# Decode attention over a long KV cache on one core: K in 16 KB rows, K and V on one transfer queue, a third V buffer

## The chip, the cores and the metric

One core of a Trainium2 chip. The metric is the device time of one execution in microseconds; medians of several executions are given. The before and after kernels were profiled in the same state, and no run of this case was in the slow state, besides three of the four of one failed experiment (10).

## The reference, cut to what matters

```python
B, Sq, D = 8, 4, 448
Hq, Hkv, Sk, Dh = 16, 8, 8192, 256          # bf16 throughout
q = (x @ wq) split into heads                # [B, Hq, Sq, Dh]
scores = einsum("bhqd,bhkd->bhqk", q, k) * Dh**-0.5     # k, v repeated twice over the heads
p = softmax(scores); o = einsum("bhqk,bhkd->bhqd", p, v)
out = o.reshape(B, Sq, Hq * Dh) @ wo
```

There are 64 pairs of batch and kv head ("heads" below). Each brings 4 MB of K and 4 MB of V that are read once: 537 MB in all, for 8 queries a head. So it is a streaming problem.

## The kernel before

Per head, TensorE transposes K in 16 groups of 512 keys (T), VectorE and ScalarE copy the transposed group out of PSUM (E), and TensorE multiplies it with the queries (QK, 3 groups later). A head behind, the softmax runs in small steps (D1 to D5, A1, P3 to P5), and then PV multiplies V with the probabilities.

```python
# SP: K in 16 slots of 512 KB, 4 KB a partition
for KGi in range(NH * 8):
    if n >= 1: eng.wait_ge(sem_T, 2 * (KGi - RK) + 2)        # slot consumed
    eng.dma_start(Kring[slot][:], k_cache[b, hkv]...[:, kg * 8 : (kg + 1) * 8, :]).then_inc(sem_kslot[slot], 16)
...
# ACT: V, two buffers, two transfers of 2 MB, 16 KB a partition
def Vdma(i):
    if i >= 2: eng.wait_ge(sem_pmisc, pm(i - 2, 4))          # PV of head i-2 done
    for q in range(2): eng.dma_start(Vbuf[i % 2][...], ...).then_inc(sem_v[i % 2], 16)
...
# TensorE: order of work
for G in range(NG + LAG):
    T(G); QK(G - LAG)
    # from group 9 of the next head on: PV of the last head, in pieces of 18 to 20 matmuls
```

Of the kernel before, what the change touches and what calls it, by code (L numbers as in the profile page):

```python
# [10 lines left out]
TG = 16  # L11
NG = NH * TG
KG_PER_HEAD = 8
RK = 16
RT = 6
NTB = 4
LAG = 3
SCALE = DH ** -0.5
NV_DMA = 2
# [12 lines left out]
def bass_standalone__gqa_block_cached__sampling_kernel(  # L32
# [24 lines left out]
    def dm(j, k):  # L57
        return 8 * j + k

    def pm(j, k):  # L60
        return 4 * j + k

    PV_SLOTS = {9: (0, 10), 10: (10, 19), 11: (19, 28), 12: (28, 37), 13: (37, 46), 14: (46, 55), 15: (55, 64)}

    with ExitStack() as ctx:
        Kring = [ctx.enter_context(nc.sbuf_tensor(f"Kr{s}", [128, 8, DH], bf16)) for s in range(RK)]
        Vbuf = [ctx.enter_context(nc.sbuf_tensor(f"Vb{s}", [128, NCH, DH], bf16)) for s in range(2)]
        KT = [ctx.enter_context(nc.sbuf_tensor(f"KT{s}", [128, 1024], bf16)) for s in range(RT)]
        wq_sb = ctx.enter_context(nc.sbuf_tensor("wq_sb", [128, 4, 2048], bf16))
        wo_sb = ctx.enter_context(nc.sbuf_tensor("wo_sb", [128, 32, D], bf16))  # L70
# [17 lines left out]
        tb16 = [tbank[t][:, :].bitcast(bf16) for t in range(NTB)]  # L88
        Sbank = [ctx.enter_context(nc.psum_tensor(f"Sb{t}", [128, 512], fp32)) for t in range(2)]
        misc = ctx.enter_context(nc.psum_tensor("misc", [128, 512], fp32))  # L90
        proj = ctx.enter_context(nc.psum_tensor("proj", [128, 512], fp32))
        misc16 = misc[:, 0:128].bitcast(bf16)
        S1_16 = Sbank[1][:, 0:64].bitcast(bf16)

        def pmaxT_ap(jp):
            return misc16[0:8, jp * 128 : (jp + 1) * 128]

        def bcast_ap(jp):
            return misc[:, 128 + jp * 8 : 128 + jp * 8 + 8]

        def oacc_ap(jp):
            return misc[:, 192 + jp * 16 : 192 + jp * 16 + 16]

        sem_kslot = [ctx.enter_context(nc.semaphore(f"sem_kslot{s}")) for s in range(RK)]
        sem_v = [ctx.enter_context(nc.semaphore(f"sem_v{s}")) for s in range(2)]
# [8 lines left out]
        sem_wqA = ctx.enter_context(nc.semaphore("sem_wqA"))  # L114
        sem_wqB = ctx.enter_context(nc.semaphore("sem_wqB"))
# [15 lines left out]
        @block.sync  # L131
        def _(eng):
            for KGi in range(NH * KG_PER_HEAD):
                i, kg = divmod(KGi, KG_PER_HEAD)
                hkv, b = _head(i)
                slot = KGi % RK
                n = KGi // RK
                if n >= 1:
                    eng.wait_ge(sem_T, 2 * (KGi - RK) + 2)
                src = k_cache[b, hkv].rearrange("(p c) d -> p c d", p=128)[:, kg * 8 : (kg + 1) * 8, :]  # L140
                eng.dma_start(Kring[slot][:], src).then_inc(sem_kslot[slot], 16)
            eng.wait_ge(sem_fin, 1)
            eng.dma_start(out.flatten_outer_dims(), out_sb[:]).then_inc(sem_out, 16)
            eng.wait_ge(sem_out, 16)

        @block.gpsimd
        def _(eng):
            eng.dma_start(x_sb[:], x.flatten_outer_dims()).then_inc(sem_x, 16)
            eng.dma_start(
                wq_sb[:, 0:3, :], wq[0:384, 0:2048].rearrange("(dc p) n -> p dc n", p=128)  # L150
            ).then_inc(sem_wqA, 16)
            eng.dma_start(wq_sb[0:64, 3, :], wq[384:448, 0:2048]).then_inc(sem_wqA, 16)
# [7 lines left out]
            eng.wait_ge(sem_qproj, 1)  # L160
            eng.dma_start(
                wq_sb[:, 0:3, :], wq[0:384, 2048:4096].rearrange("(dc p) n -> p dc n", p=128)
            ).then_inc(sem_wqB, 16)
            eng.dma_start(wq_sb[0:64, 3, :], wq[384:448, 2048:4096]).then_inc(sem_wqB, 16)
            eng.dma_start(wo_sb[:], wo.rearrange("(k p) n -> p k n", p=128)).then_inc(sem_wo, 16)

        @block.tensor
        def _(eng):
# [12 lines left out]
            def qproj(X):  # L181
                eng.wait_ge(sem_wqA if X == 0 else sem_wqB, 32)
# [3 lines left out]
                for hl in range(8):  # L186
                    for hf in range(2):
                        r = hl * 2 + hf
                        for dc in range(4):
# [3 lines left out]
                                wq_sb[0:w, dc, hl * 256 + hf * 128 : hl * 256 + (hf + 1) * 128],  # L193
# [5 lines left out]
            def outproj(hkv):  # L199
                eng.wait_ge(sem_dmisc, dm(hkv * B + B - 1, DM_D6))  # L200
                if hkv == 0:
                    eng.wait_ge(sem_wo, 16)
                    eng.wait_ge(sem_qt, 2)
                for hrep in range(2):
                    for hf in range(2):
# [4 lines left out]
                            wo_sb[:, k, :],  # L210
                            start=(k == 0), stop=(k == 31),
                        )
                if hkv == HKV - 1:
                    ins.then_inc(sem_outp, 1)

            def T(G):
                i, g = divmod(G, TG)
                KGi = i * KG_PER_HEAD + g // 2
                slot = KGi % RK
                if G % 2 == 0:  # L220
                    eng.wait_ge(sem_kslot[slot], 16 * (KGi // RK + 1))
                if G >= NTB:
                    s_, cnt = esem(G - NTB)
                    eng.wait_ge(s_, cnt)
                tb = tb16[G % NTB]
                for jj in range(4):
                    cc = (g % 2) * 4 + jj
                    for half in range(2):
                        r = jj * 2 + half
# [8 lines left out]
            def QK(G):  # L238
                i, g = divmod(G, TG)
                hkv, b = _head(i)  # L240
                s_, cnt = esem(G)
                eng.wait_ge(s_, cnt)
                if g == 0:
                    if i >= 2:
                        eng.wait_ge(sem_dmisc, dm(i - 2, DM_D5A))
# [8 lines left out]
                for jj in range(4):  # L254
                    c = g * 4 + jj
                    for half in range(2):
                        r = jj * 2 + half
# [8 lines left out]
            def P3(j):  # L266
                jp = j % 2
                eng.wait_ge(sem_dmisc, dm(j, DM_D1))
                if j >= 1:
                    eng.wait_ge(sem_dmisc, dm(j - 1, DM_D6))  # L270
                eng.matmul(pmaxT_ap(jp), pmax_sb[jp][:, 0:8], ident[:, :], is_transpose=True).then_inc(sem_pmisc, 1)  # L271

            def P4(j):
                jp = j % 2
                eng.wait_ge(sem_dmisc, dm(j, DM_D3))
# [7 lines left out]
            def PV(j, c0, c1):  # L283
                jp = j % 2
                hkv, b = _head(j)
                if c0 == 0:
                    eng.wait_ge(sem_v[jp], 16 * NV_DMA * (j // 2 + 1))
                    if j >= 1:
                        eng.wait_ge(sem_dmisc, dm(j - 1, DM_D6))
                ins = None  # L290
                for idx in range(c0 * 2, c1 * 2):
# [3 lines left out]
                        Vbuf[jp][:, c, half * 128 : (half + 1) * 128],  # L295
# [3 lines left out]
                if c1 == NCH:  # L299
                    ins.then_inc(sem_pmisc, 1)  # L300

            for G in range(NG + LAG):
                i, g = divmod(G, TG)
                j = i - 1
                if G < NG:
                    T(G)
                if G == 2:
                    qproj(0)
                if G == 16:
                    qproj(1)  # L310
                if G >= LAG:
                    QK(G - LAG)
                if j >= 0 and j < NH:
                    if g == 4:
                        P3(j)
                    elif g == 6:
                        P4(j)
                    elif g == 9:
                        P5(j)
                    if g in PV_SLOTS:  # L320
                        c0, c1 = PV_SLOTS[g]
                        PV(j, c0, c1)
                    if g == 2 and j >= B and (j % B) == 0:
                        outproj(j // B - 1)
            j = NH - 1
            P3(j)
            P4(j)
            P5(j)
            for g in range(9, 16):
                c0, c1 = PV_SLOTS[g]  # L330
                PV(j, c0, c1)
            outproj(HKV - 1)

        @block.vector
        def _(eng):
# [29 lines left out]
            def D2D3(j):  # L365
                jp = j % 2
                eng.wait_ge(sem_pmisc, pm(j, 1))
                eng.tensor_reduce(gmax_sb[0:8, jp : jp + 1], pmaxT_ap(jp), AX.X, ALU.max).then_inc(sem_dmisc, 1)  # L368
                eng.wait_ge(sem_dmisc, dm(j, DM_D2))
# [4 lines left out]
            def D4(j):  # L374
                jp = j % 2
                eng.wait_ge(sem_pmisc, pm(j, 2))
                eng.tensor_copy(bcast_sb[jp][:, :], bcast_ap(jp)).then_inc(sem_dmisc, 1)
                eng.wait_ge(sem_dmisc, dm(j, DM_D4A))
# [9 lines left out]
            def D5(j):  # L388
                jp = j % 2
                eng.wait_ge(sem_pmisc, pm(j, 3))  # L390
# [3 lines left out]
                eng.wait_ge(sem_dmisc, dm(j, DM_D5A))  # L394
                eng.reciprocal(linv_sb[jp][:, :], lsum_sb[jp][:, :]).then_inc(sem_dmisc, 1)  # L395

            def D6(j):
                jp = j % 2
                hkv, b = _head(j)
                eng.wait_ge(sem_pmisc, pm(j, 4))  # L400
                eng.wait_ge(sem_dmisc, dm(j, DM_D5B))
# [12 lines left out]
            for G in range(NG + TG):  # L414
                i, g = divmod(G, TG)
                j = i - 1
                if G < NG and not evac_is_act(G):
                    E_dve(G)
                if G == 3:
                    qt_evac(0)  # L420
                if G == 20:
                    qt_evac(1)
                if 0 <= j < NH:
                    if g == 1 and j >= 1:
                        D6(j - 1)
                    if g == 3:
                        D1(j)
                    elif g == 5:
                        D2D3(j)
                    elif g == 7:  # L430
                        D4(j)
                    elif g == 10:
                        D5(j)
            D6(NH - 1)
            eng.wait_ge(sem_outp, 1)
            eng.tensor_copy(out_sb[:, :], proj[0:32, 0:D]).then_inc(sem_fin, 1)

        @block.scalar
        def _(eng):
# [6 lines left out]
            def A1(j):  # L446
                jp = j % 2
                eng.wait_ge(sem_dmisc, dm(j, DM_D4))
                if j >= 2:
                    eng.wait_ge(sem_pmisc, pm(j - 2, 4))  # L450
                eng.activation(PT[jp][:, :], Ssub[jp][:, :], ACTF.Exp, scale=SCALE).then_inc(sem_A1, 1)  # L451

            def Vdma(i):
                hkv, b = _head(i)
                if i >= 2:
                    eng.wait_ge(sem_pmisc, pm(i - 2, 4))
                src = v_cache[b, hkv].rearrange("(p c) d -> p c d", p=128)
# [43 lines left out]
```

## Time and profile before

| | before |
|---|---|
| median time | 1356.8 us (13 runs, 1356.2 to 1358.9) |
| span of the profiled run | 1354.9 us |
| packets on the transfer engines | 94,272 |
| TensorE waits for K | 114.1 us |
| TensorE waits called issue | 63.7 us (34.4 + 16.9 + 12.4) |

TensorE's waits called issue are idle time in which it waited for nothing that the profile shows. The prediction below shows most lines of this profile. One more view is needed later, a window early in the run (length, then busy time and count of PE, PEld, DVE, ACT and POOL, then the granted clock, the busy share of the 16 transfer engines, and GB/s):

```profile
68.00:200.00 132.00, 111.44 (x2473) 107.97 (x2471) 69.83 (x131) 29.74 (x32) 0.00 (x0) 0.79 1.02 415
```

A busy share over 1 means that packets of one engine overlap in the record. This detail turns out to matter.

### The profile page before, as it was taken

What the parts mean: (1) busy time and instruction counts of PE and PEld (TensorE: products, weight loads), DVE (VectorE), ACT (ScalarE), POOL (GpSimd) and SP (SyncE); (2) the same over time, 40 slices, a digit from 0 to 9 for tenths busy, and PEclk for the clock granted to TensorE, in tenths of its full rate; (3) what the DMA queues carried; (4) which work ended last, traced back from release to release, by engine and by line L of the source; (5) the groups of instructions that cost most, each with busy time, mean ns of one, the idle gap of its engine ahead of it and who ended that gap; (6) DMA issues with size and microseconds to landing.
All of it is one profiled execution on the core that took longest, in us unless ns stands there. A gap on an engine that the chain in (4) does not pass through costs nothing.

```text
span 1354.9 us, 54067 instructions
## 1 busy us (share of the span) xinstructions
PE 1116.6 (82%) x24932; PEld 1071.0 (79%) x24932; DVE 693.0 (51%) x1291; ACT 296.7 (22%) x321; POOL 5.9 (0%) x13
## 2 busy tenths in 40 slices
PE   3888798888897887987878878888888887988886
PEld 3788787788787877877877878887887877878876
DVE  1454554554554654554545545545545545545544
ACT  0121221222222222222222212212212222122221
POOL 1000000000000000000000000000000000000000
PEclk9877887877878877877878878878877878777877
DMA  9999999999999999999999999999999999999994
GB/s 368 394 415 414 417 416 414 418 417 413 418 411 410 417 409 411 419 404 412 413 411 411 415 406 415 413 407 416 406 411 419 410 407 415 411 413 411 411 390 163
DMA packets 94272, 547.76 MB, mean 404 GB/s; under 512 B 10352, under 2 KB 10416, under 8 KB 77664
## 3 DMA queue, kind: packets, MB, share of 16 engines
q1 hardware_dynamic: 73776, 268.50, 50.1%
q10 hardware_dynamic: 18432, 268.44, 47.0%
q0 software_dynamic: 1840, 7.37, 1.5%
q8 instruction: 197, 3.23, 1.0%
q14 instruction: 27, 0.22, 0.0%
HBM read 544.24 MB, written 0.03 MB: 402 GB/s over the span
## 4 chain that ended last, share of the span: by engine, by line
DMA 73%; PE 23%; issue 2%; DVE 1%; ACT 1%; POOL 0%; SPq 0%; ACTq 0%; POOLq 0%
DMA Kr<-in_k_cache_dram 70%; PE tb L230 13%; PE misc L293 5%; PE Sb L258 3%; DMA wq_sb<-in_wq_dram 3%; PE proj L191 1%; PE proj L207 1%; ACT PT L451 0%; DVE KT L356 0%; PE Sb L281 0%; DVE diag L370 0%; DVE gmax L368 0%; PE misc L276 0%; ACT KT L444 0%; PE misc L271 0%
## 5 line engine op out<-in xcount | busy, mean ns | idle before, releaser
L230 PE MATMUL tb<-ident,Kr 128*128 128x128 bf16 x8192 | 766.9, 249 | 126.9 <-DMA Kr<-in_k_cache_dram 114.1
L356 DVE COPY KT<-tb 128x1024 bf16<-128x1024 bf16 x768 | 526.8, 690 | 625.9 <-PE tb L230 619.8
L230 PEld LDWEIGHTS tb<-ident,Kr 128*128 128x128 bf16 x8192 | 575.6, 111 | 145.1 <-DMA Kr<-in_k_cache_dram 120.3
L444 ACT ACTIVATE KT<-tb 128x1024 bf16<-128x1024 bf16 x256 | 262.1, 1024 | 1044.6 <-PE tb L230 1044.6
L258 PE MATMUL Sb<-QT_sb,KT 128*128 128x8 bf16 x8192 | 373.4, 169 | 17.1 <-issue 16.9
L258 PEld LDWEIGHTS Sb<-QT_sb,KT 128*128 128x128 bf16 x8192 | 349.5, 102 | 17.3 <-issue 17.2
L293 PE MATMUL misc<-PT,Vb 128*128 128x8 bf16 x8192 | 277.2, 167 | 34.4 <-issue 34.4
L293 PEld LDWEIGHTS misc<-PT,Vb 128*128 128x128 bf16 x8192 | 249.4, 99 | 42.6 <-issue 38.4
L381 DVE TENSOR_TENSOR Ssub<-Sb,bcast 128x512 f32<-128x512 f32 x64 | 44.3, 691 | 2.2
L391 DVE TENSOR_REDUCE lsum<-Sb 128x8 f32<-128x512 f32 x64 | 43.5, 680 | 1.4 <-PE Sb L281 1.4
L361 DVE TENSOR_REDUCE pmax<-Sb 128x8 bf16<-128x512 f32 x64 | 43.6, 681 | 0.7 <-PE Sb L258 0.6
L451 ACT ACTIVATE PT<-Ssub 128x512 bf16<-128x512 f32 x64 | 39.8, 622 | 3.3 <-DVE Ssub L381 3.3
L281 PE MATMUL Sb<-PT,ones_bf 128*128 128x512 bf16 x64 | 25.3, 396 | 12.0 <-ACT PT L451 12.0
L276 PE MATMUL misc<-diag,ones_bf 8*128 8x8 bf16 x64 | 11.2, 174 | 25.5 <-DVE diag L370 25.5
L276 PEld LDWEIGHTS misc<-diag,ones_bf 8*128 8x128 bf16 x64 | 5.8, 90 | 31.3 <-DVE diag L370 31.2
L281 PEld LDWEIGHTS Sb<-PT,ones_bf 128*128 128x128 bf16 x64 | 6.1, 96 | 17.5 <-ACT PT L451 17.5
L191 PE MATMUL proj<-xT_sb,wq_sb 128*128 128x32 bf16 (+1 forms) x128 | 10.8, 197 | 10.9 <-DMA wq_sb<-in_wq_dram 10.9
L191 PEld LDWEIGHTS proj<-xT_sb,wq_sb 128*128 128x128 bf16 (+1 forms) x128 | 8.3, 107 | 13.6 <-DMA wq_sb<-in_wq_dram 11.3
L368 DVE TENSOR_REDUCE gmax<-misc 8x1 f32<-8x128 bf16 x64 | 17.2, 269 | 0.4 <-PE misc L271 0.4
L370 DVE TENSOR_SCALAR diag<-ident,gmax 8x8 bf16<-8x8 bf16 x64 | 13.9, 217 | 2.2
L271 PE MATMUL misc<-ident,pmax 128*8 128x128 bf16 x64 | 14.2, 222 | 0.8 <-DVE pmax L361 0.8
L395 DVE RECIPROCAL linv<-lsum 128x8 f32<-128x8 f32 x64 | 13.0, 203 | 2.2
(25 smaller groups left out, 48.7 us busy)
## 6 DMA issues: line engine op xcount, KB each, us to landing
Kr<-in_k_cache_dram SPq DMA_DIRECT2D x512, 512.0 KB, 26.6
Vb<-in_v_cache_dram ACTq DMA_DIRECT2D x128, 2048.0 KB, 15.7
wo_sb<-in_wo_dram POOLq DMA_DIRECT2D x1, 3584.0 KB, 41.5
wq_sb<-in_wq_dram POOLq DMA_DIRECT2D x2, 1536.0 KB, 17.3
wq_sb<-in_wq_dram POOLq DMA_DIRECT2D x2, 256.0 KB, 18.7
x_sb<-in_x_dram POOLq DMA_DIRECT2D x1, 28.0 KB, 6.5
out_dram<-out_sb SPq DMA_DIRECT2D x1, 28.0 KB, 1.5
```

The lines of the kernel that those rows point to most:

```text
L191: ins = eng.matmul(proj[:, r * 32 : (r + 1) * 32], wq_sb[0:w, dc, hl * 256 + hf * 128 : hl * 256 + (hf + 1) * 128], xT_sb[0:w, dc, :], sta ...
L230: ins = eng.matmul(tb[:, r * 128 : (r + 1) * 128], Kring[slot][:, cc, half * 128 : (half + 1) * 128], ident[:, :], is_transpose=True,)
L258: ins = eng.matmul(Sb[:, c * 8 : (c + 1) * 8], kt[:, r * 128 : (r + 1) * 128], QT_sb[:, hkv, half, b, :], start=(half == 0), stop=(half == 1),
L281: eng.matmul(Sbank[jp][:, 0:512], ones_bf[:, :], PT[jp][:, :]).then_inc(sem_pmisc, 1)
L293: ins = eng.matmul(oacc_ap(jp)[:, half * 8 : (half + 1) * 8], Vbuf[jp][:, c, half * 128 : (half + 1) * 128], PT[jp][:, c * 8 : (c + 1) * 8 ...
L356: eng.tensor_copy(KT[G % RT][:, :], tb16[G % NTB][:, :]).then_inc(sem_Edve, 1)
L361: eng.tensor_reduce(pmax_sb[jp][:, :], Sbank[jp][:, :].rearrange("p (c q) -> p q c", q=8), AX.X, ALU.max).then_inc(sem_dmisc, 1)
L368: eng.tensor_reduce(gmax_sb[0:8, jp : jp + 1], pmaxT_ap(jp), AX.X, ALU.max).then_inc(sem_dmisc, 1)
L381: eng.tensor_tensor(Ssub[jp][:, :].rearrange("p (c q) -> p c q", q=8), Sbank[jp][:, :].rearrange("p (c q) -> p c q", q=8), bcast_sb[jp][:, ...
L391: eng.tensor_reduce(lsum_sb[jp][:, :], Sbank[jp][:, :].rearrange("p (c q) -> p q c", q=8), AX.X, ALU.add).then_inc(sem_dmisc, 1)
L444: eng.activation(KT[G % RT][:, :], tb16[G % NTB][:, :], ACTF.Copy).then_inc(sem_Eact, 1)
L451: eng.activation(PT[jp][:, :], Ssub[jp][:, :], ACTF.Exp, scale=SCALE).then_inc(sem_A1, 1)
```

## The change

The intent: larger pieces a packet and a transfer, one queue whose order is chosen by hand, and enough buffers that the one queue doesn't block. Cut to its core:

```diff
-KG_PER_HEAD = 8
-RK = 16
+K_CH = 32                      # a K slot: 2 MB, 16 KB a partition
+RK = 4
+NVB = 3                        # V buffers (2 before)
-NTB = 4
+NTB = 3                        # PSUM banks for T
+PV_PARTS = 16                  # PV in 16 parts of 8 matmuls, over two heads
...
         @block.sync
+            for KGi in range(NH * KG_PER_HEAD):
+                Kdma(KGi)
+                if (v_next < 2 and KGi == 1 + 2 * v_next) or (v_next >= 2 and KGi == KG_PER_HEAD * v_next + KG_PER_HEAD + v_next // 62):
+                    Vdma(v_next)                 # waits for the PV of head v_next - 3
+                    ... Wodma(wo_next)           # wo in eight pieces
+                    v_next += 1
+            ... the last V loads stand behind the last K
...
         @block.scalar                           # wq whole, staged in the third V buffer
+            eng.dma_start(wq_stage[:, 0:3, :], wq[0:384, :]...).then_inc(sem_wq, 16)
```

The rest is one schedule function that all engines walk, with counters in place of formulas for the waits. It also puts the small softmax pieces into the PSUM bank that T gave up, and the second q projection in group 6 instead of 16.

## The prediction

> **What bounds the kernel now.** I read the page from the top: busy shares, slices, queues, chain. The engine shares name no bound (PE 82% busy, everything else half or less), but the slices do.
>
> ```profile
> PE 1116.6 (82%) x24932; PEld 1071.0 (79%) x24932; DVE 693.0 (51%) x1291; ACT 296.7 (22%) x321; POOL 5.9 (0%) x13
> ...
> DMA  9999999999999999999999999999999999999994
> GB/s 368 394 415 414 417 416 414 418 417 413 418 411 410 417 409 411 419 404 412 413 411 411 415 406 415 413 407 416 406 411 419 410 407 415 411 413 411 411 390 163
> ...
> q1 hardware_dynamic: 73776, 268.50, 50.1%
> q10 hardware_dynamic: 18432, 268.44, 47.0%
> q0 software_dynamic: 1840, 7.37, 1.5%
> q8 instruction: 197, 3.23, 1.0%
> ```
>
> The DMA row is full from the first slice to the last but one, and the rate is flat near 413 GB/s. Queue q1 is K (issued by SP), q10 is V (issued by ACT): the same 268 MB each, but K takes 50.1% of the 16 engines' span and V 47.0%. K comes in 512 KB transfers (4 KB a partition), V in 2 MB transfers (16 KB a partition). The four shares add up to 99.6%.
>
> Second view, the chain that ended last, and third, what the TensorE waited for:
>
> ```profile
> DMA 73%; PE 23%; issue 2%; DVE 1%; ACT 1%; POOL 0%; SPq 0%; ACTq 0%; POOLq 0%
> ```
>
> ```profile
> PE tb L230 <- DMA Kr<-in_k_cache_dram: 114.1, 63, 6.3
> PE misc L293 <- issue: 34.4, 26, 3.0
> PE misc L276 <- DVE diag L370: 25.5, 63, 0.9
> ```
>
> The chain is a K transfer for most of the run, and PE waits for K about once per head (63 times, 114.1 us). So this is a transfer-bound kernel with PE as a near second. The fourth view is the windows, for steady state and the end:
>
> ```profile
> 200.00:600.00 400.00, 335.61 (x7566) 321.72 (x7563) 209.94 (x390) 90.25 (x98) 0.00 (x0) 0.82 1.01 414
> 600.00:1000.00 400.00, 334.72 (x7524) 323.42 (x7525) 208.76 (x387) 89.73 (x97) 0.00 (x0) 0.80 1.01 411
> ...
> 1318.00:1320.00 2.00, 1.42 (x35) 1.43 (x36) 0.00 (x0) 0.00 (x0) 0.00 (x0) 0.85 0.45 184
> 1320.00:1322.00 2.00, 2.00 (x47) 2.00 (x45) 0.27 (x1) 1.02 (x1) 0.00 (x0) 0.50 0.70 254
> ```
>
> The last two numbers are DMA share and GB/s. Steady state is saturated (1.01). Near 1318 the queues run partly dry: the last V may only be issued once a buffer is free, at 1320.9. After 1332 the share falls away and the last K lands at 1338.7; the remaining 16 us are a serial tail:
>
> ```profile
> 1338.78 1.03 PE tb L230 x8
> ...
> 1342.89 0.70 DVE pmax L361
> ...
> 1346.97 3.41 PE misc L293 x128
> ...
> 1350.63 1.69 PE proj L207 x4
> ...
> 1352.34 0.61 DVE out_sb L436
> ```
>
> **What the Trainium skill says.** "DMA: Bandwidth & Descriptors", section "Issuing engines are not separate DMA queues": transfers of SP, ACT and GpSimd run on the same 16 engines and interleave. The trace agrees: two busy queues sum to 97.1%, not to 194%. So putting V on the SP queue should cost no bandwidth. The same page, "Why small descriptors are slow (HBM only)", gives a fixed overhead per packet; it quantifies it for small ones only. This trace shows that a 4 KB packet still pays something (50.1% against 47.0%). The same page, "Where 436 GB/s comes from", puts the ceiling at 435 GB/s and a measured 16 MB load at 425; the 413 here leaves at most 5% and plausibly 3%. "TensorE: Matmul & The Clock Gate", section "Part 1: The HAM clock gate (the "warmup" mystery)", says that the clock halves after an idle window of some 3.4 us. The trace shows the clock at 0.50 after waits for K, for example from 600 to 606 us after 2.5 us of idling, so a part of PE's 82% is made by the waiting itself.
>
> **The change, part by part.**
> (1) K in 2 MB transfers, 16 KB a partition, four slots: the same 8 MB of ring. The engine time of one K transfer is now 0.501 x 1354.9 x 16 / 512 = 21.2 us, so 84.9 for 2 MB; V needs 0.470 x 1354.9 x 16 / 128 = 79.6 for the same bytes. If K takes V's cost, it saves 5.3 x 128 / 16 = 42 us of saturated transfer time (3.1%). This is on the path that sets the end, since the DMA row has no gap to hide it in.
> (2) V moves from the ACT queue to the SP queue and gets a third buffer. Round robin between a 4 KB and a 16 KB stream ends. V(v) is queued after the first half of K of head v+1; its wait (the PV of head v-3) and that of the K transfer ahead of it come true at about the same group, so the in-order SP queue should not block itself. By my count 14 MB, some 34 us, are queued when PE starts the second half of a head. The third buffer lets the last V be issued a head earlier: the dry spot at 1316 to 1324 goes, worth (0.18+0.55+0.30+0.11) x 2 = 2.3 us.
> (3) wq arrives at once on the ACT queue in 8 KB rows instead of in two loads of GpSimd's; wo in eight loads of 0.46 MB. Same 7.37 MB; the 896 B rows of wo cost more packets, the 8 KB rows of wq fewer. I book 20 us as now (q0's 1.5%). q projection starts near 28 us instead of 24.8 (wq now shares each engine with 16 KB packets), but the second one no longer waits until 46.5. The first 20 MB are issued without waiting for PE, 49 us of work, so transfers go on meanwhile; I book 1 us of gaps.
> (4) PE: the same 24,932 matmuls; PV is cut into 16 parts of 8 and spread over two heads, T has three PSUM banks instead of four. QK(G-3) right after T(G) needs the same evacuation that T(G) now waits for, so a bank less costs little: two other groups, about 2 us, lie between, against 0.69 (DVE) or 1.02 us (ACT) for a copy. No cost booked while transfers bound.
> (5) The end. The last transfer is now V of head 63, not K. Scores, softmax and PV of head 62 fit under the 20 us of the last two V loads. After it come PV x128 (3.4), D6 (0.2), output projection (1.7), copy (0.6), store (about 1.5) and the hand-overs: from 1346.8 to 1354.9, 8.1 us, against 16.1 now. Saves 8 us.
>
> **Sum.** Packet time after: K 0.47 + V 0.47 + instructions 0.01 = 0.95 x 1354.9 = 1287, plus 20 for wq and wo: 1307 us. Shares over 1 mean that packets overlap a little: all of 1349.5 us of packet time went in some 1330 us of saturated time, a factor of 1.014. 1307 / 1.014 = 1289. Plus 1.6 start, 1 gap, 4 for engines that finish unevenly (about 5.4 now: 1332 to 1340 at a mean share of a third), 1 for the last landing, 8.1 tail: span 1305. Timed runs are 1.7 above the span: 1307 us, 3.7% less.
>
> **Rivals.**
> A. The rate is limited by the memory and not by packets; 16 KB packets change nothing. Then 547.8 MB at 413 is 1326, plus start and unevenness 6 and tail 8, plus 1.7: 1342 less what the slow first slices gain, some 1335 to 1342; within 2%. Against it: V's bytes cost 6% less engine time than K's in the same run, side by side. For it: the two streams were interleaved, and a share of busy time is not a rate.
> B. PE becomes the bound. PE is busy 1116.6 us and waits about 105 us for things other than transfers and the start: 1222 us, below 1289. It has 5% in hand, and less waiting keeps the clock up. If NTB 3, the spread PV or longer instruction stalls cost it 1 us more per head, PE needs 1286: 1310 to 1325.
> C. The single in-order queue blocks: K behind a V that waits for PV, or 4 MB of V ahead of a K that PE wants. Then the DMA row shows 8s and the rate dips each head. A stall of 1 us per head is 64 us: 1370, slower. The 34 us of queued work speaks against it.
>
> **Range and chances.** My number rests on one measured ratio (K against V) and a tail read from the trace. Below it lies a pure 16 KB stream faster than V's share says (425 GB/s: 1289 for all bytes, so about as booked) and no unevenness: 1294. Above lie half the gain of (1) lost (+21) or B (+15). Time 1307, 80% in 1292 to 1330. The 2% line is 1329.4: faster 0.86, same 0.11, slower 0.03.
>
> **What would show each step.** (1) The K and V share of the one queue near 94% of the old span in packet time, some 37,000 packets instead of 92,000, GB/s rows of 420 to 426. Rows still at 413 make rival A right. (2) No slice under 9 before the last; SP's own waits on PV short. A DMA share under 0.97 in steady windows is rival C. (4) PE still waiting for K in total 50 us or more, about once per head; waits near zero mean B. (5) The last landing some 8 us before the end, followed by 128 PV matmuls, projection, copy and store. Wrong altogether if the time is above 1330.

## The result, and the profile after

The changed kernel takes 1325.6 us (median of 8 runs, 1325.0 to 1330.5) against 1356.8: 2.3% less. The ratio is 0.9771, 95% interval 0.9762 to 0.9781; ratios here are the mean time of one kernel's fast runs over that of the other's of the same rounds, so they are not quite the ratio of the medians. The time lies inside the range that was given, near its upper end: 31 us were gained where 50 were predicted. The question is where the other 18 to 19 us stayed.

The page of the changed kernel: span, engine shares, the slices of DMA share and rate, the queues, and the chain that ended last.

```profile
span 1324.5 us, 53249 instructions
...
PE 1106.5 (84%) x24932; PEld 1054.5 (80%) x24932; DVE 699.5 (53%) x1291; ACT 296.7 (22%) x321; POOL 0.8 (0%) x7
...
DMA  9999999999999999999999999999999999999994
GB/s 370 413 428 425 422 424 424 426 423 424 424 425 426 423 426 423 424 425 425 425 422 411 415 425 420 422 422 420 418 426 421 409 420 420 424 407 407 415 406 184
DMA packets 41883, 547.68 MB, mean 413 GB/s; under 512 B 4288, under 2 KB 8448, under 8 KB 8448
...
q1 hardware_dynamic: 41136, 540.59, 97.1%
q8 instruction: 195, 3.19, 1.0%
q10 hardware_dynamic: 528, 3.70, 0.7%
...
DMA 51%; PE 44%; issue 4%; DVE 1%; ACT 0%; ACTq 0%
```

The rate is at 422 to 428 from the third slice to the twenty-first, as foreseen, and then dips again and again, to 406 at the lowest. The shares add up to 98.8% of 1324.5, which is 1308.6 us of packet time; the prediction had 1307. So the amount of transfer work was right, and the time that it took was not.

Windows of the changed kernel, early, middle, late, and at the end:

```profile
68.00:200.00 132.00, 114.88 (x2652) 110.35 (x2650) 74.71 (x138) 31.93 (x35) 0.00 (x0) 0.83 1.01 425
200.00:600.00 400.00, 344.09 (x7793) 329.03 (x7791) 218.48 (x403) 92.67 (x101) 0.00 (x0) 0.81 1.01 425
...
1000.00:1280.00 280.00, 241.02 (x5375) 230.23 (x5373) 150.70 (x275) 63.07 (x68) 0.00 (x0) 0.79 0.99 414
1300.00:1310.00 10.00, 8.13 (x205) 7.69 (x202) 6.65 (x15) 3.59 (x4) 0.00 (x0) 1.00 0.50 210
```

From 1300 to 1310 the share is 0.50 and the rate is half: half of the transfer engines have finished, the others have not. (Of the last V load's landings, eight came by 1299.6 and eight from 1312.8 to 1315.0.) From the fences of before, the early rate rose from 415 to 425, 2.4%, and not the 3.1% that the shares of K and V had promised.

TensorE's waits in the changed kernel (waiter, releaser, us in total, times, longest):

```profile
PE tb L342 <- DMA Kr<-in_k_cache_dram: 74.1, 38, 3.9
PE misc L405 <- issue: 43.3, 40, 2.3
PE Sb L370 <- issue: 36.6, 31, 2.0
PE proj L304 <- DMA Vb<-in_wq_dram: 20.9, 1, 20.9
PE tb L342 <- issue: 20.3, 25, 1.7
```

TensorE still waits for K, and transfers are still the largest part of the chain, though it is 51% now and was 73%. But the waits called issue have grown from 63.7 us to 100.2 (43.3 + 36.6 + 20.3). And the end, from the timeline (start, length, what):

```profile
1316.04 3.42 PE L405 MATMUL misc<-PT,Vb 128*128 128x8 bf16 x123
...
1320.30 1.67 PE L320 MATMUL proj<-wo_buf,oT_all 128*32 128x448 bf16 x4 [0.27 <-DVE oT_all L512]
...
1322.65 0.36 SPq L267 DMA_DIRECT2D out_dram<-out_sb  x1
```

The last V landed at 1315.0 by the trace's landing records, and the span ends 9.5 us later: the tail is as predicted (8.1 and 1 for the landing). So the miss is in the landing: 1315 where the sum of the prediction (1289 + 1.6 + 1 + 4 + 1) had 1297.

**A reading that the views do not print.** The Trainium skill ("DMA: Bandwidth & Descriptors", section "🔬 Why a DMA increments its semaphore by 16 and not by 1") says that a transfer runs on up to 16 engines and that each counts the semaphore up when its own part has landed. The trace records these 16 times for each transfer, so one can see how far the first engine is ahead of the last. For one of the four K slots of the changed kernel (the other three show the same), worked out from those records:

```
transfer          first of 16   8th     9th     last    first to last
K of head 2           62.7      63.0    63.1    64.7        2.0 us
K of head 18         378.9     384.0   388.6   390.1       11.1
K of head 34         694.3     703.4   713.6   714.8       20.5
K of head 62        1266.8    1267.4  1283.2  1284.6       17.8
```

The engines drift apart steadily until the leaders are some 20 us ahead; then the leaders have nothing queued and stand still until the last engine frees a slot. That is where the dips in the rate begin (about 700 us), and it is why half of the engines end 15 us early. The pace of the last engine never changes: 20.32 us a head from head 2 to 34, and (1284.6 - 714.8) / 28 = 20.35 from 34 to 62. The first engine needs (694.3 - 62.7) / 32 = 19.74. The end is set by the last engine, not by the mean that a rate or a share shows.

### The profile page after: what moved, and what is told of

Its sections match the earlier page's. It is cut to its first block, busy times and chain, and to the rows that moved or that the text cites. A ratio compares the mean times of both kernels' runs of the same rounds, so it can differ in the third digit from the quotient of the medians.

```text
span 1324.5 us, 53249 instructions
## 1 busy us (share of the span) xinstructions
PE 1106.5 (84%) x24932; PEld 1054.5 (80%) x24932; DVE 699.5 (53%) x1291; ACT 296.7 (22%) x321; POOL 0.8 (0%) x7
## 2 busy tenths in 40 slices
DMA packets 41883, 547.68 MB, mean 413 GB/s; under 512 B 4288, under 2 KB 8448, under 8 KB 8448
## 4 chain that ended last, share of the span: by engine, by line
DMA 51%; PE 44%; issue 4%; DVE 1%; ACT 0%; ACTq 0%
DMA Kr<-in_k_cache_dram 48%; PE tb L342 25%; PE misc L405 8%; PE Sb L370 7%; DMA Vb<-in_wq_dram 2%; PE Sb L391 1%; PE proj L304 1%; DVE KT L456 1%; PE proj L320 1%; PE misc L381 0%; PE misc L386 0%; ACT KT L546 0%; DVE diag L470 0%; DVE gmax L468 0%; DVE pmax L461 0%
## 5 line engine op out<-in xcount | busy, mean ns | idle before, releaser
L342 PE MATMUL tb<-ident,Kr 128*128 128x128 bf16 x8192 | 755.7, 246 | 94.8 <-DMA Kr<-in_k_cache_dram 74.1
L342 PEld LDWEIGHTS tb<-ident,Kr 128*128 128x128 bf16 x8192 | 567.7, 110 | 106.9 <-DMA Kr<-in_k_cache_dram 77.9
L370 PE MATMUL Sb<-QT_sb,KT 128*128 128x8 bf16 x8192 | 373.6, 169 | 44.1 <-issue 36.6
L405 PE MATMUL misc<-PT,Vb 128*128 128x8 bf16 x8192 | 351.9, 167 | 43.6 <-issue 43.3
L370 PEld LDWEIGHTS Sb<-QT_sb,KT 128*128 128x128 bf16 x8192 | 347.1, 102 | 47.8 <-issue 43.3
L405 PEld LDWEIGHTS misc<-PT,Vb 128*128 128x128 bf16 x8192 | 286.0, 98 | 68.4 <-issue 61.8
L391 PE MATMUL Sb<-PT,ones_bf 128*128 128x512 bf16 x64 | 35.1, 548 | 0.2 <-ACT PT L553 0.2
L304 PE MATMUL proj<-xT_sb,Vb 128*128 128x32 bf16 (+1 forms) x128 | 10.8, 198 | 20.9 <-DMA Vb<-in_wq_dram 20.9
L304 PEld LDWEIGHTS proj<-xT_sb,Vb 128*128 128x128 bf16 (+1 forms) x128 | 8.4, 108 | 23.4 <-DMA Vb<-in_wq_dram 21.1
L386 PE MATMUL misc<-diag,ones_bf 8*128 8x8 bf16 x64 | 11.4, 178 | 5.5 <-DVE diag L470 5.4
L470 DVE TENSOR_SCALAR diag<-ident,gmax 8x8 bf16<-8x8 bf16 x64 | 13.9, 217 | 2.3
L477 DVE COPY bcast<-misc 128x8 f32<-128x8 f32 x64 | 9.7, 151 | 7.7 <-PE misc L386 7.7
## 6 DMA issues: line engine op xcount, KB each, us to landing
wo_buf<-in_wo_dram SPq DMA_DIRECT2D x8, 448.0 KB, 36.4
```

Of the source, the lines that this page charges most:

```text
L304: ins = eng.matmul(proj[:, r * 32 : (r + 1) * 32], wq_view(X, dc)[0:w, hl * 256 + hf * 128 : hl * 256 + (hf + 1) * 128], xT_sb[0:w, dc, :] ...
L342: ins = eng.matmul(tb[:, r * 128 : (r + 1) * 128], Kring[slot][:, cc, half * 128 : (half + 1) * 128], ident[:, :], is_transpose=True,)
L370: ins = eng.matmul(Sb[:, c * 8 : (c + 1) * 8], kt[:, r * 128 : (r + 1) * 128], QT_sb[:, hkv, half, b, :], start=(half == 0), stop=(half == 1),
L391: eng.matmul(Sbank[jp][:, 0:512], ones_bf[:, :], PT[jp][:, :]).then_inc(sem_pmisc, 1)
L405: ins = eng.matmul(oacc_ap(jp)[:, half * 8 : (half + 1) * 8], Vbuf[jv][:, c, half * 128 : (half + 1) * 128], PT[jp][:, c * 8 : (c + 1) * 8 ...
```

## The experiments

Each is the changed kernel with one edit, except where it says otherwise. Four were wrong in their result on purpose and are marked; the others gave the right result.

### 1. K again in 4 KB rows, all else as after

```diff
-                eng.dma_start(Kring[slot][:], src).then_inc(sem_kslot[slot], 16)
+                for q in range(4):
+                    eng.dma_start(Kring[slot][:, q*8:(q+1)*8, :], src[:, q*8:(q+1)*8, :]).then_inc(sem_kslot[slot], 16)
```

> The changed kernel with the same 2 MB K slots, the same order and the same single queue, but each slot filled by four transfers of 512 KB, 4 KB a partition (65,536 K packets again instead of 16,384). Packet-cost theory: K needs 5% to 6% more engine time again, time 1350 to 1358, the rate in the slices back to 410 to 416. Rival A (the memory's rate bounds, packets do not matter): 1323 to 1329 and slices at 425.

Measured: 1351.5 us, ratio to before 0.9957 (0.9942 to 0.9972), so 25.9 us slower than the change. The early window and the packets of this run:

```profile
68.00:200.00 132.00, 110.83 (x2590) 108.03 (x2598) 72.65 (x135) 31.25 (x34) 0.00 (x0) 0.82 1.02 416
...
DMA packets 97182, 547.73 MB, mean 406 GB/s; under 512 B 10432, under 2 KB 14592, under 8 KB 80128
```

The packet theory holds and rival A falls: rate and share go back to those of before (416, 1.02). With everything else of the change in place, the rows are worth 26 us, and the rest without the rows about 5. The 26 us are 55,299 packets (97,182 - 41,883) on 16 engines: 7.5 ns a packet. (The number of transfers grew with that of the packets, so the two are not told apart.) The share stays at 1.02 on a single queue, so the overlap in the record belongs to the short packets, not to two queues: short packets look dearer in busy time than they are in elapsed time.

### 2. K in 8 KB rows

The same edit with two transfers of 1 MB for each slot.

> The changed kernel with each K slot filled by two transfers of 1 MB, 8 KB a partition (32,768 K packets). If the cost is a fixed time per packet, a third of the extra packets of the 4 KB case (16,384 instead of 49,152) cost a third of its 26 us: 1331 to 1337. If 8 KB is already enough: 1324 to 1328.

Measured: 1335.6 us, 10.0 above the change, for 18,433 packets more (60,316): 8.7 ns each. The cost goes with the count of packets.

### 3. V in 32 KB rows

```diff
-NV_DMA = 2
+NV_DMA = 1
```

> The changed kernel with V in one transfer of 4 MB a head, 32 KB a partition (8,192 V packets instead of 16,384). If a packet costs some 9 ns beyond its bytes, 8,192 packets fewer save 4 to 5 us: 1319 to 1323. If 16 KB is at the limit: 1324 to 1328. If longer packets hold up the instruction fetch: over 1328.

Measured (4 runs): 1327.7 us, ratio 0.9788 (0.9773 to 0.9802). No gain, though the packets fell to 32,666. Three of TensorE's waits in this run:

```profile
PE misc L405 <- issue: 59.4, 85, 2.7
PE Sb L370 <- issue: 44.3, 36, 2.2
...
PE tb L342 <- issue: 35.0, 34, 2.3
```

The waits called issue sum to 138.7 us against 100.2. Experiment 6 tells what they are, and 8 comes back to this one.

### 4. The kernel before with 16 KB rows alone

```diff
 # kernel before
-KG_PER_HEAD = 8
-RK = 16
+K_CH = 32
+KG_PER_HEAD = NCH // K_CH
+RK = 4
```

> The kernel before with only K's geometry changed (four slots of 2 MB, 16 KB a partition); V still on its own queue with two buffers, the old tail. Packet-cost theory: most of the gain comes with this alone, 1330 to 1337; the dry spot before the last V and the 16 us tail after the last K stay, so not all of it. If the gain comes from the single queue, the third V buffer or the order of the end: 1350 to 1357.

Measured: 1346.5 us, ratio 0.9927 (0.9899 to 0.9955): a gain of about 10 us (6 to 14 by the interval), not 20 to 27. A miss of the expectation. The chain that ended last and the largest waits of TensorE:

```profile
PE 65%; DMA 16%; issue 11%; DVE 5%; ACT 3%; POOL 0%; ACTq 0%; POOLq 0%
```

```profile
PE misc L295 <- issue: 59.5, 46, 3.1
PE tb L232 <- issue: 42.0, 33, 2.9
PE Sb L260 <- issue: 33.0, 29, 2.7
...
PE tb L232 <- DMA Kr<-in_k_cache_dram: 5.2, 1, 5.2
```

TensorE hardly waits for K any more (5.2 us). By these sums it is the bound here: busy 1112.8 and issue 134.5 are 1247 of the 1346.5, and the rest is mostly its waits at the start (29.5), for the softmax and for V. The faster rows alone run into TensorE, so the parts of this change need one another. (The page also has 287 GB/s in its second slice against 424 later, a hole of some 11 us at the start. How much of it reaches the end was not tested; TensorE waits for K only 5.2 us after it.)

### 5. V on ACT's queue again, with the three buffers

```diff
-                    Vdma(v_next)                 # in SP's loop
+            # ACT, in group 8 of head h:
+                    if g == 8 and 2 <= h + 1 < NH: Vdma(h + 1)
```

> The changed kernel with V issued on ACT's queue instead of SP's, same buffers. If two queues overlap packets and one queue loses that overlap (busy share 1.007 against 1.016 of before; the conversion factor of the prediction), this is faster than the change: 1314 to 1321 and a rate near 430. If the queue does not matter: 1322 to 1330.

Measured: 1337.5 us, ratio 0.985 (0.9832 to 0.9868), 12 us slower than the change. Both expectations missed; the prediction's own statement that V on SP's queue costs nothing had made me expect nothing here either way. TensorE's waits:

```profile
PE misc L381 <- issue: 59.4, 75, 2.6
PE Sb L346 <- issue: 50.3, 39, 2.6
PE tb L318 <- issue: 42.6, 33, 2.4
...
PE tb L318 <- DMA Kr<-in_k_cache_dram: 7.5, 4, 3.9
```

Again TensorE is the bound: 152.3 us of issue and 7.5 of K. Two theories: the last K now shares the engines with the last V (it landed at 1307 instead of 1295, and the serial rest of the last head hangs on it), or the stalls. I looked at the 76 idle stretches of TensorE above 0.9 us in this trace: 73 of them ended 1 to 2 us after an instruction packet ended, and such a packet comes only every 6.6 us. So most of what is called issue in this run is TensorE waiting for its own instructions, which travel on the same transfer engines. The Trainium skill ("Runtime: NRT & Kernel Launch", section "🔬 Instruction fetch mechanics") says that instructions come in 16 KB blocks of 256, and that the cost is mostly hidden. The blocks agree: in the page of the change, 195 of them are 49,920 instructions, and TensorE has 49,864 (weight loads counted). That it is hidden doesn't hold here. The stalls are not the whole of it: TensorE is also busy for longer than in the change, 1129.3 us against 1106.5, at a granted clock of 0.781 against 0.815.

### 6. Fewer instructions for TensorE (wrong result on purpose)

```diff
-                    for half in range(2):                    # QK
+                    for half in range(1):
-                for idx in range(part * per, (part + 1) * per):      # PV
+                for idx in range(part * per, (part + 1) * per, 4):
```

> Wrong result on purpose: the changed kernel with half of the QK matmuls and a quarter of the PV matmuls, all transposes kept, so about 58% of TensorE's instructions. Theory 1 (half of the transfer engines lag because they also carry the instruction fetch): fetch packets fall from 195 to about 115, the two halves of the engines end some 9 us apart instead of 15, the last V lands near 1307 instead of 1315, span 1310 to 1316. Theory 2 (half of the engines are slower in themselves): still 15 us apart, last V near 1315, span 1319 to 1323 (a tail shorter by some 3 us).

Measured: 1307.0 us (2 runs, 1305.9 and 1308.1), ratio 0.963. Rates and instruction packets:

```profile
GB/s 373 425 424 427 425 426 425 427 425 426 427 426 426 425 427 424 428 427 421 429 424 426 426 426 425 427 426 426 424 427 426 427 425 425 425 427 424 429 387 243
...
q8 instruction: 116, 1.90, 0.6%
```

The dips are gone. By the landing records, the same K slot has 1.8 us from first to last engine at head 2 and 13.2 at head 34: a growth of 11.4 us where the change has 18.5, a factor of 0.62 for 0.59 of the instruction packets. The first engine's pace is the same (19.72 us a head against 19.74), the last one's fell from 20.32 to 20.07, and 0.25 x 64 is 16 us, which is what the last V gained (1298.6 against 1315.0). Theory 1 holds: the lag of the last engines goes with the instruction packets, some 0.58 us a head in the change. Its details missed: the lag is spread over the engines here instead of two halves, and the span (1304.1) is 6 us below the theory's range. By itself this run leaves a rival: the cut takes away matmuls and their reads too, and not only instruction packets.

**The packet records settle it.** They do not name the engine, but on one engine a data packet begins 3 or 4 ns before the one ahead of it ends, so the chain can be followed. In the changed kernel a data packet of 16 KB takes 0.61 us; an instruction packet takes 1.05, and the data packet behind it ends 2.16 us after the instruction packet began (in the 136 of 181 cases, from 100 to 1290 us, where exactly one data packet fits). So the engine loses some 1.55 us to each. From 350 to 1260 us, 47 of the 96 with this mark could be followed to the landing of a K slot on one half of the engines alone: 46 among the eight that land last, 1 among the eight that land first. Data packets picked at random and followed in the same way were 387 times among the last and 407 times among the first. The instruction packets thus sit on the late half, and the sizes fit: 195 x 1.55 / 8 engines / 64 heads is 0.59 us a head against 0.58 measured, and 116 packets give 0.35 against 0.35 (20.07 - 19.72).

### 7. Two V buffers on the one queue

```diff
-NVB = 3
+NVB = 2                        # wq gets a buffer of its own
```

> The changed kernel with two V buffers instead of three (wq gets its own buffer), all else the same, so V(v) waits for the PV of head v-2 and stands in the one in-order queue ahead of K. Rival C of the prediction (the single queue blocks) then comes true: busy share under 0.97 in steady windows, 1340 to 1370. If the depth of the queue still covers the wait: 1324 to 1330.

Measured: 1336.3 us, ratio 0.9848 (0.9832 to 0.9865), below the range of the rival and above that of the other theory. The slices:

```profile
GB/s 377 419 304 424 424 421 416 421 415 424 417 415 425 421 416 415 410 427 411 428 417 419 412 416 421 419 425 424 411 414 423 417 423 420 412 426 406 424 423 240
```

The loss is one hole in the third slice: (425 - 304) / 425 x 33.3 = 9.5 us, at the start, when the loop fills and V of head 2 blocks the queue until the first PV is done. After that the pace is that of the change (40.6 us for two heads, from the landing records). So the third buffer is worth about 10 us, all at the start, and the rival's steady loss did not come: the busy share is 1.00 in the windows from 200 us on. One more thing can be seen in these records. From head 4 on, a K slot has only 3 to 6 us between its first and last engine here, with the same 195 instruction packets. With two buffers the first engines don't run ahead, and yet the last engine's pace is the same. So a small lead does not mean that the lag is gone.

### 8. Are two queues or long rows slow in themselves? (wrong results on purpose)

The edits of experiment 6 on the kernels of 5 and 3.

> Wrong result on purpose: V on ACT's queue, with the same cut of TensorE's instructions to 58% as in the earlier run that took 1307 us with one queue. If two queues cost time only because TensorE stalls for its instructions and becomes the bound, the cost is gone here: 1303 to 1311. If two queues of 16 KB packets cost transfer time in themselves: 1316 to 1322.

> Wrong result on purpose: V at 32 KB a partition, with TensorE's instructions cut to 58%. If 8,192 packets fewer do save 9 ns each per engine and the full kernel lost it to longer instruction stalls: 1301 to 1304. If packets over 16 KB save nothing: 1305 to 1309.

Measured: V on ACT's queue 1320.6 us, V in 32 KB rows 1305.3, against 1307.0 with one queue and 16 KB. The first number falls in the range of "transfer time in themselves", but the trace says otherwise: all transfers had landed at 1299.4, as with one queue (1298.6). What differs is the order: V had run ahead, and the last transfer to land was the last K. TensorE sat idle for it just before:

```profile
1289.43 1.03 PE L318 MATMUL tb<-ident,Kr 128*128 128x128 bf16 x8 [20.64 <-DMA Kr<-in_k_cache_dram]
```

The rest of the last head, 19 us, came after that. The 32 KB rows give some 1.7 us without the stalls (1304.9 to 1306.2 against the two runs of experiment 6, 1305.9 and 1308.1), less than the 4 to 5 that 9,217 packets at 8 ns would save: its steady windows show 427 to 428 GB/s against 426, but its second slice stands at 363 against 425.

### 9. Two queues, with the last two V loads behind the last K

```diff
+            Vdma(NH - 2, eng)      # on SP, after its loop over K
+            Vdma(NH - 1, eng)
```

Once with all instructions and once with the cut of experiment 6 (wrong result on purpose):

> The kernel with V on ACT's queue, but the last two V loads issued on SP's queue behind the last K. If two queues cost 12 us because the last K shares the engines with the last V (it landed at 1307 instead of 1295, and the serial rest of the last head hangs on it): 1324 to 1331. If they cost 12 us because TensorE stalls longer for its instructions between two streams of 16 KB packets (stalls called issue of 152 us against 100): 1334 to 1340.

> Wrong result on purpose: V on ACT's queue except the last two V loads, which stand on SP's queue behind the last K, with TensorE's instructions cut to 58%. Without the instruction stalls, what two queues cost (1320.6 against 1307.0) is then the order at the end alone (the last K landed last, at 1299, with its serial rest of 19 us still to come): 1304 to 1311. If something else in two queues costs it: 1315 to 1322.

Measured: 1335.7 us with all instructions, 1308.0 with fewer. Without the instruction stalls the order at the end explains the whole difference between one queue and two (1320.6 to 1308.0, against 1307.0). With all instructions, the last K lands at 1293.8, early enough, and the last V at 1313.5, before that of the change (1315.0). The kernel still needs 1335.7, with 153.7 us of issue waits (65.2 + 52.1 + 36.4) and 9.1 us of waiting for K: TensorE is late, not the transfers. So the one queue of the change pays twice: it fixes the order at the end, and it keeps TensorE from becoming the bound. Either alone loses about 10 to 14 us: 13.6 by the order where the instructions are cut (1320.6 - 1307.0), 10.1 by TensorE where the order is kept (1335.7 - 1325.6). That longer stalls make TensorE late is not shown. Its issue waits and waits for K together are 162.8 us here and 174.3 in the change, so a stall may only stand where a wait for K would have been; what is longer is its busy time, 1122.9 us against 1106.5, at a granted clock of 0.788 against 0.815. The cut of experiment 6 takes away stalls and busy time alike. Why the instruction packets are later beside two streams of 16 KB packets stays open: with 4 KB and 16 KB rows on one queue the stalls were 98.8 us, with 16 KB alone 100.2, so the size of the packets ahead is not the whole of it, and in the first of these TensorE waited for K longer too (143.7 us against 74.1).

### 10. Moving work from one half of the engines to the other

Every second head, the last V half in cuts of 112, 8 and 8 partitions instead of 128.

> Correct result. In the changed kernel every second head's last V half is cut by partitions into 112 + 8 + 8, so that the two cuts of 8 partitions run on half of the transfer engines only; this moves about 0.3 us of work per head from one half of the engines to the other. If the receiving half is the one that runs ahead, the halves end 19 us closer at most, the last V lands 5 to 9 us earlier and the time is 1316 to 1321. If the receiving half is the one that lags, its lag doubles: 1338 to 1348. If the lag is not a matter of load per engine: 1323 to 1329.

Measured: 1706.8 us in the one fast run, 1737 to 1752 in three slow ones; the result was right. None of the theories: the transfer rate fell to 315 GB/s in steady windows, some 12 us for every cut ((1706.8 - 1325.6) / 32). It tells nothing about the lag, and why cuts by partition cost this much was not followed up.

No experiment gave a correct kernel faster than the change.

## Why the prediction was right or wrong, point by point

- **Transfers bound the kernel, and 16 KB rows are the gain: right.** Rival A (the memory's rate) is refuted by experiments 1 and 2. Packet time came to 1308.6 us where 1307 was summed.
- **The step that was mis-sized: "all of 1349.5 us of packet time went in some 1330 us of saturated time, a factor of 1.014", applied to the changed kernel as it stood.** The factor came from short packets that overlap in the record. With long ones the busy share in 20 us stretches of steady state is 1.007 and not 1.015, so 1308.6 us of packet time need about 1300 saturated, not 1289: 10 us of the 18. Seen by the term itself: part (1) was booked with 41 us elapsed (42 of packet time) and measures 26 (experiment 1). The same fault lies in "5.3 us for 2 MB", which is 12 ns for each of the 432 packets more (packets of semaphores included: 576 against 144), where experiments 1 and 2 show 7.5 and 8.7. (The gains of single parts do not add up to the whole, since each experiment keeps the other parts.)
- **The other 8 us: "4 for engines that finish unevenly".** The last transfer lands at 1315.0. Less the start of 1.6 and the saturated time of 1299.5 (1308.6 / 1.007), 13.9 us remain for idle leaders, gaps and landing, where 6 (4 + 1 + 1) had been booked. The prediction spread the instruction packets evenly, as 1% of a mean; experiment 6 shows that the late half of the engines pays for them, and that the last engine sets the end. On such an engine they cost 195 x 1.55 / 8, some 38 us of the run, where the 1% had some 13.5. The same drift was there before the change: 20 us from the first to the last engine of a K slot at head 16.
- **V on SP's queue costs no bandwidth: right, but too small a thought.** Nothing is lost in rate, and some 12 us are won by the order at the end and by a TensorE that is less late (experiments 5, 8, 9). The prediction had booked neither.
- **The third buffer, booked with the dry spot of 2.3 us:** worth about 10 us, at the start and not at the end (experiment 7).
- **TensorE: right in the sum, wrong in the reason for its margin.** It waited for K for 74.1 us, over the 50 that were named, though 38 times and not once a head. Rival B named "longer instruction stalls" and they came: 100.2 us. In the changed kernel the waits for K that remain leave room for them; in experiments 4, 5 and 9, with 5 to 9 us of waiting for K, TensorE with its stalls is the bound. The prediction's aside on the clock needs a correction: it names an idle window of some 3.4 us beside 2.5 us of idling. In the clock record the fall to 0.50 comes at 599.2, which is 1.5 us into that wait (597.7 to 600.2), so here a shorter idle time was enough.
- **wq and the end:** q projection began at 33.3 us instead of 28, at no visible cost. The tail after the last landing is 9.5 us against 9.1 booked: right.

## What to carry to other kernels

A share of busy time or a mean rate over 16 transfer engines is not a finish time: look for the engine that ends last, and test how much a busy record is worth in elapsed time by changing the number of packets alone. In a streaming kernel with tens of thousands of matmuls, the instruction stream is itself a stream on the same engines; here it slowed the engines that land last and it stalled TensorE. Where two streams feed one pipeline, try them on one queue, and choose the order at the end so that the transfer with the longest serial rest lands first: that alone was worth 13.6 us here.

## What the Trainium skill lacked or had wrong

- "DMA: Bandwidth & Descriptors" ("Why small descriptors are slow (HBM only)") speaks of small packets. At 4 and 8 KB a packet still costs 7.5 to 8.7 ns beyond its bytes: 25.9 and 10.0 us of some 1330 in experiments 1 and 2.
- The same page ("Issuing engines are not separate DMA queues") says that the issuing engine only saves issue time. For the rate this holds (1308.0 us with two queues against 1307.0, with fewer instructions and the order kept). But the choice was worth 12 us to the kernel: 1337.5 with two queues against 1325.6 with one, by the order of the last transfers and by a later TensorE.
- "Runtime: NRT & Kernel Launch" ("🔬 Instruction fetch mechanics") calls the fetch mostly hidden. TensorE's waits called issue are 100.2 us in the change and 152.3 with two queues, where 73 of its 76 long idle stretches ended 1 to 2 us after an instruction packet.
- No page that I read says that instruction packets fall on a part of the transfer engines and set these back: some 1.55 us a packet on eight of the 16, 20.5 us from first to last by head 34, growing with the number of instruction packets (195 against 116: 18.5 against 11.4 us over 32 heads).
- No page that I read gives a cost for cutting a transfer to 112 + 8 + 8 partitions: some 12 us for each cut in experiment 10.
